# Set attention and SoLU MLP in one kernel: the finish and the norm on ScalarE and GpSimd, the output weights spread by TensorE, and batch 0's turned x stored once all x is in

## The chip, the cores and the metric

The kernel runs on one core of a Trainium2 chip, as one hand-ordered program. The time is device time in microseconds of one execution; three runs of the kernel before took 1380.73 to 1383.75 us, median 1381.25.

The engines are named as the profile names them: PE is TensorE's matmul stream and PEld its weight loads, DVE is VectorE, ACT ScalarE, POOL GpSimd, SP SyncE, which here only issues transfers.

## What is computed

Four batches of 12608 rows of 128 values go through an attention block with 32 inducing points and then through a SoLU MLP with a layer norm. Everything is float32; the weights `w_in`, `w_out` and `g_ln` arrive as 64-bit floats.

```python
def mab(q, kv):                                  # softmax attention, scale 1/sqrt(128)
    s = scale * (q @ kv.transpose(0, 2, 1)); s = s - s.max(-1, keepdims=True)
    a = np.exp(s); a /= a.sum(-1, keepdims=True) + 1e-09
    return a @ kv
h = mab(I, x)            # 32 points look at all rows of a batch
x1 = mab(x, h)           # every row looks at the 32 pooled points
h = x1 @ w_in                                    # 128 -> 1024
e = np.exp(h - h.max(-1)); solu = h * e / (e.sum(-1) + 1e-09)
ln = (solu - mean(solu)) / np.sqrt(var(solu) + 1e-06) * g_ln
out = ln @ w_out                                 # 1024 -> 128
```

## The kernel before

**Tiles and stages.** A tile is 128 rows; a batch has 99 tiles (the last one half full), so there are 396 tiles in all. Groups of four tiles share one product with the output weights; five groups share one finish, so there are 100 groups and 20 finishes.

- `p1(b, k)` reads a chunk of x (up to 12 tiles in batch 0, 16 later), turns it on PE (L614 in batch 0, L583 later), copies it out (`xT`, L561, L593), stores the turned chunk to the DRAM tile `xd` (L624), and updates a running softmax of the 32 points over all rows. `combine(b)` makes the pooled points `h4` and `hs = h4 @ w_in` (L767 to L793).
- `p2(b, j)` takes up to 16 tiles, reads the turned x back from `xd` (L818), makes the scores of the rows against the pooled points (L833), their softmax numerators (L840 to L852), turns those (L875, L889) and computes `rn`, minus the reciprocal of their sums: L908 sums, L911 negates and adds 1e-9, L914 inverts.
- `main` with `mm1` multiplies a tile of numerators with `hs` (L1013). `soft` evicts the 128x1024 product from PSUM on DVE (L1054), takes the exponential on ACT (L1065), multiplies on POOL (L1069), squares on ACT for the norm's sums (L1080) and turns the result on DVE (L1093). `products` and `driver` multiply the turned groups with the output weights `wc` on PE (L1136), in two halves (`w`) that can run beside each other and beside L1013. `evacuate` copies the result out on DVE or ACT (L1159).
- `floor` carries the row sums through DRAM into the layout of the result (L1110, L1118). `finish(b, f)` makes the norm's factor for five groups: L1185 to L1189 on DVE, a logarithm and an exponential on ACT (L1192, L1193), L1196 to L1198 on DVE, all on tiles of 128x20 values. Then POOL scales five groups (L1205) and `stored` writes them (L1217, L1231).

**The start.** `rounded` turns a 64-bit weight matrix into float32 with integer operations on DVE (L417 to L426), one conversion on ACT (L428), multiplications and additions on POOL (L431, L433), a mask on DVE (L435) and a multiplication by it on POOL (L438). `weights_in` and `weights_out` use the same five work buffers (`conv`, part of the `EU` buffers and `hn_b[1]`), one after the other. `weights_out` then scales by the gain (ACT, L460), subtracts the mean of the rows (PE L469, DVE L474) and copies each 32-row block of the result to four places with 16 transfers (L490), which makes `wc`.

**What sets the order.** A planner (`Planner.run`) steps through a model of the engines at build time and emits each instruction when the model has its inputs ready, the lowest priority number first. Each engine's queue is thus a fixed order. The constants at the top (`PR_...`, `P1_...`, `WOUT`, `WIN`, `LATE`) are priorities, and `HN_MORE`, `EUS` and `MINE` share out buffers: four spare buffers of 128x1024 are split between `HN` (evicted products) and `EU` (exponentials), and `MINE` bounds how many first products may be under way.

**Banks.** In the start the eight PSUM banks are `bank_e`, in the locks `EARLY_TR` and `EARLY_PB`. `handover` closes them and gives out four double banks `H` once all of batch 0's `p1` and `hs` are done. Until then nothing that needs `H` can run, neither `mm1` nor, before the change, `p2(0, 0)`.

Of the kernel before, what the change touches and what calls it, by code (L numbers as in the profile page):

```python
# [55 lines left out]
HN_MORE = 3  # L56
RAWS = 2
FILL = 400
FIRST = 4
LATE = -15  # L60
P1_FROM = 3
P1_GO = -20
P1_STEP = 11
P2_AHEAD = 35
P2_START = 35
PR_EX = -2
PR_EV = -20
PR_FI = 40
PR_G2 = 4
PR_HN = -4  # L70
PR_MU = 1
PR_SQ = 1
PR_TU = 4
# [177 lines left out]
def set_attention_then_solu_kernel(ctx: ExitStack, tc: tile.TileContext, x, inducing, w_in, w_out, g_ln, out):  # L251
# [9 lines left out]
    start = min(FIRST, some[0][1] - 1)  # L261
    at_groups = [[(0, start), (start, some[0][1] - start)] + some[1:]] + [some] * (NB - 1)
# [66 lines left out]
    HW = Lock([(buf([C, P], f"h4_{i}"), buf([P, FF], f"hs{i}")) for i in range(2)])  # L329
# [75 lines left out]
    def rounded(dst, src, w, after, free, prio):  # L405
        flat = w[0].bitcast(U32)
        raw = flat.rearrange("p (f two) -> p f two", two=2)
        bits, rest, power, mag = (v.bitcast(U32) for v in w[1:])
        lo, hi = raw[:, :, 0], raw[:, :, 1]
        to = flat if len(src.shape) == 2 else flat.rearrange("p (k d) -> p k d", k=KC)  # L410
        got = (yield after["raw"]) if after else None
        d = yield dma(P * FF * 8, lambda: nc.sync.dma_start(to, src), got, prio=prio)
        ts, stt = nc.vector.tensor_scalar, nc.vector.scalar_tensor_tensor
        gt, gs = nc.gpsimd.tensor_tensor, nc.gpsimd.tensor_scalar
        keep = power.bitcast(F32)
# [6 lines left out]
        a = yield Op("DVE", 1100, lambda: stt(out=bits, in0=hi, scalar=0xC0000000, in1=bits, op0=ALU.bitwise_and, op1=ALU.bitwise_or), a)  # L422
# [12 lines left out]
        k = yield Op("DVE", 602, lambda: ts(out=keep, in0=mag.bitcast(I32), scalar1=float(0x38100000), scalar2=None, op0=ALU.is_ge), g)  # L435
        plan.set(free["mag"], k)
        for c in cuts:
            g = yield Op("POOL", 1180, lambda: gt(out=dst[:, c], in0=dst[:, c], in1=keep[:, c], op=ALU.mult), g, k)  # L438
# [10 lines left out]

    def weights_out():  # L450
        wg2 = hn_b[2]
        wg = wg2.rearrange("p (k d) -> p k d", k=KC)
        g = yield from rounded(wg2, w_out.bitcast(U32).rearrange("(k p) d -> p k d", p=P), conv, conv_free, conv_end, WOUT)
# [3 lines left out]
        gd = yield dma(4096, lambda: nc.sync.dma_start(g_sb, g_ln.rearrange("(k p) -> p k", p=P)))  # L457
# [6 lines left out]
        g = [d]  # L464
        mp, rel = yield H
# [5 lines left out]
        d = yield Op("PE", KC * 215, mean, g, rel, prio=LATE)  # L471
# [54 lines left out]
    e2 = [wc_flat[:, 2 * each : 2 * each + PG0 * M], wc_flat[:, 2 * each + PG0 * M : 2 * each + 2 * PG0 * M]] + [spare[:, (5 * PG0 * C) + i * PG0 * M :][:, : PG0 * M] for i in range(2)]  # L526
# [4 lines left out]
    turned = [Event() for _ in range(NP[0])]  # L531

    def p1(b, k):
# [86 lines left out]
        yield copied  # L620

        def store():
# [3 lines left out]
            d = yield dma(n * P * C * 4, go, ready)  # L626
# [179 lines left out]
    def p2(b, j):  # L806
        s0, n = at_groups[b][j]
        A = aT_of[(b, j)]
        bank = H
        prev = []  # L810
        for k, (g0, gn) in enumerate(p1_groups[b]):
            if g0 < s0 + n and s0 < g0 + gn:
                d = yield xd_done[(b, k)]
                prev += d
        xT, rel = yield X2
        d = yield dma(
            n * P * C * 4,
            lambda: nc.sync.dma_start(xT[:, :n, :].rearrange("p s t -> p (s t)"), xT_dram[b][:, s0 * P : (s0 + n) * P]),  # L818
            rel, prev,
        )  # L820
# [17 lines left out]
        d = yield Op("PE", SWITCH + n * 60, scores, d, rel, hd)  # L838
        give(X2, xT, d)
# [17 lines left out]
        ways, copied, read = [0, 1], [], []  # L857

# [50 lines left out]
        d = yield Op(
            "DVE", 75,  # L910
            lambda: nc.vector.tensor_scalar(out=nr[:, :n], in0=nr[:, :n], scalar1=-1.0, scalar2=-1e-9, op0=ALU.mult, op1=ALU.add),  # L911
            d,
        )
# [254 lines left out]
    def finish(b, f):  # L1168
# [16 lines left out]
        de = yield small(lambda: ts(out=z, in0=S, scalar1=1e-3, scalar2=1e-12, op0=ALU.mult, op1=ALU.add), fd)  # L1185
        de = yield small(lambda: tt(out=z, in0=z, in1=z, op=ALU.mult), de)  # L1186
        d = yield small(lambda: stt(out=part, in0=total, scalar=1.0 / (FF * FF), in1=total, op0=ALU.mult, op1=ALU.mult), F["out"])  # L1187
        d = yield small(lambda: tt(out=v, in0=Q, in1=part, op=ALU.subtract), fd, d)
        d = yield small(lambda: stt(out=v, in0=v, scalar=0.0, in1=z, op0=ALU.max, op1=ALU.add), d, de)  # L1189

        def inverse():
            nc.scalar.activation(y, v, AF.Ln)  # L1192
            nc.scalar.activation(root, y, AF.Exp, scale=-0.5)  # L1193

        da = yield Op("ACT", 330, inverse, d)
        d = yield small(lambda: stt(out=z, in0=root, scalar=-0.5, in1=root, op0=ALU.mult, op1=ALU.mult), da)  # L1196
        d = yield small(lambda: tt(out=z, in0=z, in1=v, op=ALU.mult), d)  # L1197
        dy = yield small(lambda: stt(out=y, in0=z, scalar=1.5, in1=root, op0=ALU.add, op1=ALU.mult), d, da)  # L1198
# [52 lines left out]
    def handover():  # L1251
# [6 lines left out]
        done += d  # L1258
        bank_pool.__exit__(None, None, None)
# [63 lines left out]
```

## Time and profile before

| what | us |
|---|---|
| median of three runs | 1381.25 |
| the profiled execution | 1387.33 |
| its span, first to last instruction | 1385.1 |
| PE busy / PEld busy | 1236.7 / 1142.9 |
| DVE busy | 1255.2 |
| ACT busy | 1062.2 |
| POOL busy | 1072.8 |

The page gives each engine's busy time over the whole span, then groups of instructions by line, with the buffers written and read, the shape, the count, the busy time and the mean duration of one, and after a bar the idle time of the engine just before them and who ended it. "Busy" means that an instruction has begun and not ended; an instruction that sits on an engine and waits for a resource counts as busy too. PE's matmuls overlap, and one float32 matmul leaves two records, so a count of PE records per microsecond says more than its busy share. The table of stretches gives the same busy times for any part of the span, with the granted PE clock as a share of full speed.

### The profile page before, as it was taken

Reading aid. Unit: us, or ns where it says so; the run is one execution under the profiler, and the core shown is the slowest. Engines: PE = TensorE matmul, PEld = TensorE weight load, DVE = VectorE, ACT = ScalarE, POOL = GpSimd, SP = SyncE. Lnnn points to the kernel's source line nnn. Section 1 sums busy time; section 2 is a strip of 40 time slices with the busy share of each in tenths; the row PEclk is TensorE's granted clock in tenths of the full one; section 3 lists DMA queues with packets and bytes.
Section 4 is the critical chain, followed back from the end, with each engine's and each line's share of the span. In section 5 each row is a group of like instructions: output and inputs, shape, how many; then the busy total and the mean of one; then the engine's idle time right before and its main releaser. Section 6 shows DMA issues by size and latency. Waiting matters only on the chain. (4 is left out here: it accounts for less than half of the span.)

```text
span 1385.1 us, 77913 instructions
## 1 busy us (share of the span) xinstructions
PE 1236.7 (89%) x35557; PEld 1142.9 (83%) x35557; DVE 1255.2 (91%) x1882; ACT 1062.2 (77%) x2015; POOL 1072.8 (77%) x557
## 2 busy tenths in 40 slices
PE   9889999989988989899989998689998998989785
PEld 7678888978887978888878887688888887889784
DVE  5698899999999899999998999999999899999992
ACT  5588688968877877878887787578787787789681
POOL 2577587959876978878887778678788796889793
PEclk9879899999999999999999999899999999999897
DMA  9552242203231325312213324121222020201102
GB/s 365 187 162 65 82 138 65 85 17 103 60 123 50 100 65 156 87 44 55 82 45 123 117 78 125 47 88 30 67 70 73 4 70 19 63 4 43 31 16 75
DMA packets 152905, 113.58 MB, mean 82 GB/s; under 512 B 76256, under 2 KB 132608, under 8 KB 148096
## 3 DMA queue, kind: packets, MB, share of 16 engines
q1 hardware_dynamic: 152576, 108.62, 26.2%
q8 instruction: 277, 4.54, 1.4%
q14 instruction: 52, 0.43, 0.1%
HBM read 54.30 MB, written 52.18 MB: 77 GB/s over the span
## 5 line engine op out<-in xcount | busy, mean ns | idle before, releaser
L1136 PE MATMUL h<-wc,vt 32*128 32x129 f32 x25600 | 1068.9, 280 | 34.0 <-issue 17.1
L1136 PEld LDWEIGHTS h<-wc,vt 32*128 32x128 f32 x25600 | 1023.8, 191 | 71.3 <-issue 40.5
L1013 PE MATMUL h<-hs,aT 32*128 32x128 f32 x6336 | 459.6, 286 | 81.0 <-DVE spare L1054 46.6
L1069 POOL TENSOR_TENSOR eu<-hn,eu 128x1024 f32<-128x1024 f32 x197 | 463.3, 2372 | 77.4 <-ACT eu L1065 75.5
L1013 PEld LDWEIGHTS h<-hs,aT 32*128 32x128 f32 x6336 | 408.0, 196 | 109.1 <-DVE spare L1054 53.5
L1093 DVE STREAM_TRANSPOSE vt<-eu 128x1024 f32<-128x1024 f32 x330 | 402.6, 1228 | 1.3 <-POOL eu L1069 1.0
L1080 ACT ACTIVATE sq<-eu 128x1024 bf16<-128x1024 f32 x330 | 347.2, 1052 | 31.0 <-POOL eu L1069 25.5
L1069 POOL TENSOR_TENSOR eu<-spare,eu 128x1024 f32<-128x1024 f32 x133 | 313.7, 2375 | 58.8 <-ACT eu L1065 56.0
L1054 DVE TENSOR_SCALAR_CACHE_REDUCE hn<-h,rn 128x1024 f32<-128x1024 f32 x198 | 248.6, 1261 | 29.7 <-PE h L1013 20.5
L1054 DVE TENSOR_SCALAR_CACHE_REDUCE spare<-h,rn 128x1024 f32<-128x1024 f32 x198 | 248.8, 1260 | 25.8 <-PE h L1013 23.2
L1065 ACT ACTIVATE eu<-hn,nm 128x1024 f32<-128x1024 f32 x197 | 224.9, 1143 | 25.4 <-DVE hn L1054 19.6
L1069 POOL TENSOR_TENSOR spare<-spare 128x1024 f32<-128x1024 f32 x65 | 154.2, 2372 | 31.6 <-ACT spare L1065 31.4
L1065 ACT ACTIVATE eu<-spare,nm 128x1024 f32<-128x1024 f32 x133 | 151.9, 1143 | 24.8 <-DVE spare L1054 20.4
L1205 POOL TENSOR_TENSOR spare<-spare,fin 128x512 f32<-128x512 f32 x100 | 101.0, 1042 | 46.7 <-issue 32.1
L1159 ACT COPY spare<-h 128x258 f32<-128x258 f32 (+1 forms) x119 | 43.7, 371 | 112.1 <-PE h L1136 111.6
L1093 DVE STREAM_TRANSPOSE vt<-spare 128x1024 f32<-128x1024 f32 x66 | 80.8, 1225 | 0.3 <-POOL spare L1069 0.2
L1065 ACT ACTIVATE spare<-spare,nm 128x1024 f32<-128x1024 f32 x65 | 74.3, 1143 | 4.1 <-DVE spare L1054 3.7
L1080 ACT ACTIVATE sq<-spare 128x1024 bf16<-128x1024 f32 x66 | 69.3, 1050 | 4.9 <-POOL spare L1069 3.8
L1080 ACT ACTIVATION_READ_ACCUMULATOR sq<-eu 128x1 f32 x330 | 62.7, 190 | 0.0
L1159 DVE COPY spare<-h 128x258 f32<-128x258 f32 (+1 forms) x81 | 32.7, 410 | 33.1 <-PE h L1136 32.7
L583 PE MATMUL h<-ident,xn 32*128 32x32 f32 x1188 | 54.3, 227 | 6.6 <-DVE spare L1054 3.7
L845 POOL TENSOR_TENSOR s<-s,mx 128x512 f32<-128x512 f32 (+3 forms) x29 | 26.7, 922 | 42.4 <-DVE mx L842 41.3
(162 smaller groups left out, 971.5 us busy)
## 6 DMA issues: line engine op xcount, KB each, us to landing
out_dram<-spare SPq DMA_DIRECT2D x96, 256.0 KB, 3.7
xT<-xd SPq DMA_DIRECT2D x19, 1024.0 KB, 5.4
xn<-in_x_dram SPq DMA_DIRECT2D x15, 1024.0 KB, 6.6
xd<-xT SPq DMA_DIRECT2D x15, 1024.0 KB, 4.7
dl<-dd SPq DMA_DIRECT2D x396, 1.0 KB, 2.6
xd<-vt SPq DMA_DIRECT2D x7, 768.0 KB, 10.4
spare<-in_x_dram SPq DMA_DIRECT2D x5, 768.0 KB, 12.5
xT<-xd SPq DMA_DIRECT2D x5, 768.0 KB, 4.4
```

Of the source, the lines that this page charges most:

```text
L583: nc.tensor.transpose(out=tr[:, k * 512 + s * M : k * 512 + (s + 1) * M], in_=xn[r, s, :], identity=ident[r, r])
L845: lambda: nc.gpsimd.tensor_tensor(out=s2[:, :n, :], in0=s2[:, :n, :], in1=mx[:, :n].unsqueeze(2).to_broadcast([P, n, M]), op=ALU.subtract),
L1013: nc.tensor.matmul(hp[:, cols], lhsT=aT[rows, i // 2, :], rhs=hs[rows, cols], start=True, stop=True)
L1054: lambda: nc.vector.tensor_scalar(out=hn, in0=hp, scalar1=rn, scalar2=None, op0=ALU.mult, op1=ALU.min, accum_out=nm),
L1065: "ACT", 1133, lambda: nc.scalar.activation(e, hn, AF.Exp, bias=nm, scale=-1.0, accum_out=G["qe"][:, s, 1:2]), d, rel, srel,
L1069: d = yield Op("POOL", 2330, lambda: nc.gpsimd.tensor_tensor(out=e, in0=hn, in1=e, op=ALU.mult), de, prio=t + PR_MU)
L1080: "ACT", 1040, lambda: nc.scalar.activation(sq, e, AF.Square, scale=1.0 / 32.0, accum_out=G["qe"][:, s, 0:1]), d,
L1093: lambda: nc.vector.transpose(out=G["vtb"][:, : n * FF].rearrange("p (j s t) -> p j s t", j=M, s=n)[:, :, s, :], in_=e.rearrange("p (a f) ...
L1136: nc.tensor.matmul(op[:rows, a - 2 * w, : C + 1], lhsT=vt[q, k, :], rhs=wc[q, k, :], start=(k == 0), stop=(k == JB - 1))
L1159: return lambda: eng(F["raw"][:rows, i0 : i0 + 2, :], op[:rows, :, : C + 1])
L1205: return lambda: eng.tensor_tensor(out=raw, in0=raw, in1=y[:, i0 : i0 + 4].unsqueeze(2).to_broadcast([rows, 4, C]), op=ALU.mult)
```

## The change

- `finish`: the eight DVE instructions go. Squares, the clamp and two linear steps are done on ACT, two-input steps on POOL: five small ACT instructions beside the two that were there (L1192, L1193), and four on POOL.
- `p2`: the negation of the row sums (L911) is an ACT instruction.
- `rounded`: the mask and the multiplication by it become one DVE instruction; the two POOL halves go.
- `weights_out` gets work buffers of its own (`conv2`, lent by `HW`, `A4`, `AT` and `HN`), is loaded ahead of `w_in`, and replaces the 16 transfers by eight matmuls with `fold2`, which copy each 32-row block to the four places, and eight copies out of PSUM on ACT or DVE. Its mean and these products use the early banks, and `handover` waits for `wc`.
- `p1` of batch 0 stores its turned chunks only when all loads of batch 0 have landed. The first chunk of batch 0 (12 tiles) is cut for `p2` into 4 and 8 tiles that read `xT` where it is in SBUF. `p2(0, 0)` runs in the early banks and turns its numerators whole.
- Constants: `HN_MORE` 3 to 4 (seven `HN` and five `EU` buffers in place of six and six), `MINE` 2 to 3, `WINDOW_TILES` 3 to 4, and several priorities.

```diff
-HN_MORE = 3
+HN_MORE = 4
...
-PR_HN = -4
-PR_MU = 1
-PR_SQ = 1
-PR_TU = 4
+PR_HN = 0
+PR_MU = -4
+PR_SQ = 4
+PR_TU = 12
...
-WINDOW_TILES = 3
-MINE = 2
+WINDOW_TILES = 4
+MINE = 3
...
+WOUT_X = -17.5
 WOUT = -8
-WIN = -18.5
+WIN = -15.5
...
-        k = yield Op("DVE", 602, lambda: ts(out=keep, in0=mag.bitcast(I32), scalar1=float(0x38100000), scalar2=None, op0=ALU.is_ge), g)
-        plan.set(free["mag"], k)
-        for c in cuts:
-            g = yield Op("POOL", 1180, lambda: gt(out=dst[:, c], in0=dst[:, c], in1=keep[:, c], op=ALU.mult), g, k)
+        g = yield Op(
+            "DVE", 1150,
+            lambda: stt(out=dst, in0=mag.bitcast(I32), scalar=float(0x38100000), in1=dst, op0=ALU.is_ge, op1=ALU.mult), g, m,
+        )
...
-        mp, rel = yield H
+        yield turned[NP[0] - 1]
+        mp, rel = yield EARLY_PB.at(LATE)
...
-        for a in range(4):
-            for q in range(4):
-                c = yield dma(
-                    M * FF * 4,
-                    lambda: nc.sync.dma_start(rows[a * M : (a + 1) * M, :, q, :C], wg[q * M : (q + 1) * M]), d, o, issue=600, prio=LATE,
-                )
...
+            def copies():
+                for q, sp in enumerate(four):
+                    r = slice(q * M, (q + 1) * M)
+                    nc.tensor.matmul(sp, lhsT=fold2[r, :], rhs=wg2[r, k0 * C : (k0 + half) * C], start=True, stop=True)
...
+            dc = yield Op(
+                "ACT", 570, out_of(nc.scalar.copy, sp, q, k0), dp, o, prio=LATE,
+                alt=Op("DVE", 620, out_of(nc.vector.tensor_copy, sp, q, k0), dp, o, prio=LATE),
+            )
...
+            here = []
+            for e in loaded if early else ():
+                d = yield e
+                here += d
+            d = yield dma(n * P * C * 4, go, ready, here)
...
+        if b == 0 and s0 + n <= PG0:
+            rel = yield early_xT["ready"]
+            xT = early_xT["tile"][:, s0 : s0 + n, :]
+            d = rel
...
-        d = yield Op(
-            "DVE", 75,
-            lambda: nc.vector.tensor_scalar(out=nr[:, :n], in0=nr[:, :n], scalar1=-1.0, scalar2=-1e-9, op0=ALU.mult, op1=ALU.add),
-            d,
-        )
+        d = yield Op("ACT", 100, lambda: nc.scalar.activation(nr[:, :n], nr[:, :n], AF.Copy, scale=-1.0, bias=-1e-9), d)
...
-        de = yield small(lambda: ts(out=z, in0=S, scalar1=1e-3, scalar2=1e-12, op0=ALU.mult, op1=ALU.add), fd)
-        de = yield small(lambda: tt(out=z, in0=z, in1=z, op=ALU.mult), de)
-        d = yield small(lambda: stt(out=part, in0=total, scalar=1.0 / (FF * FF), in1=total, op0=ALU.mult, op1=ALU.mult), F["out"])
-        d = yield small(lambda: tt(out=v, in0=Q, in1=part, op=ALU.subtract), fd, d)
-        d = yield small(lambda: stt(out=v, in0=v, scalar=0.0, in1=z, op0=ALU.max, op1=ALU.add), d, de)
+        gt, act = nc.gpsimd.tensor_tensor, nc.scalar.activation
+        dz = yield Op("ACT", 135, lambda: act(z, S, AF.Square, scale=1e-3, bias=tiny[:rows]), fd)
+        d = yield Op("ACT", 135, lambda: act(part, total, AF.Square, scale=1.0 / FF), F["out"])
+        d = yield Op("POOL", 205, lambda: gt(out=v, in0=Q, in1=part, op=ALU.subtract), fd, d)
+        d = yield Op("ACT", 135, lambda: act(v, v, AF.Relu), d)
+        d = yield Op("POOL", 205, lambda: gt(out=v, in0=v, in1=z, op=ALU.add), d, dz)
...
+            act(z, root, AF.Square)
...
-        d = yield small(lambda: stt(out=z, in0=root, scalar=-0.5, in1=root, op0=ALU.mult, op1=ALU.mult), da)
-        d = yield small(lambda: tt(out=z, in0=z, in1=v, op=ALU.mult), d)
-        dy = yield small(lambda: stt(out=y, in0=z, scalar=1.5, in1=root, op0=ALU.add, op1=ALU.mult), d, da)
+        d = yield Op("POOL", 205, lambda: gt(out=z, in0=z, in1=v, op=ALU.mult), da)
+        d = yield Op("ACT", 135, lambda: act(z, z, AF.Copy, scale=-0.5, bias=1.5), d)
+        dy = yield Op("POOL", 205, lambda: gt(out=y, in0=z, in1=root, op=ALU.mult), d)
...
+        for e in (early_turned, wc_ready):
+            d = yield e
+            done += d
         bank_pool.__exit__(None, None, None)
```

More of the change, by code (lines that the diff above doesn't have):

```diff
@@ L260, in set_attention_then_solu_kernel @@
     some = cut(NT, AG, GS)
-    start = min(FIRST, some[0][1] - 1)
-    at_groups = [[(0, start), (start, some[0][1] - start)] + some[1:]] + [some] * (NB - 1)
+    start = min(FIRST, PG0 - 1)
+    first = [(0, start), (start, PG0 - start)]
+    at_groups = [first + [(PG0 + s, n) for s, n in cut(NT - PG0, AG, GS)]] + [some] * (NB - 1)
     NP, NG = [len(g) for g in p1_groups], len(ff_groups)
@@ L456, in weights_out @@
         give(HN, hn_b[1], g)
-        gd = yield dma(4096, lambda: nc.sync.dma_start(g_sb, g_ln.rearrange("(k p) -> p k", p=P)))
+    def weights_out():
+        gd = yield dma(4096, lambda: nc.sync.dma_start(g_sb, g_ln.rearrange("(k p) -> p k", p=P)), prio=WOUT_X)
+        wg2 = hn_b[2]
+        wg = wg2.rearrange("p (k d) -> p k d", k=KC)
+        for lock, bufs, at in ((HW, hw_b, ("raw",)), (A4, [a4_b], ("bits",)), (AT, aT_b, ("rest", "mag")), (HN, hn_b[:1], ("power",))):
+            spawn(lend(lock, bufs, *[conv2_free[k] for k in at]), WOUT)
+        g = yield from rounded(wg2, w_out.bitcast(U32).rearrange("(k p) d -> p k d", p=P), conv2, None, conv2_free, WOUT_X)
         def gain(k):
@@ L493, in weights_out, with out_of @@
-        give(HN, wg2, *spread)
-        plan.set(wc_ready, *o_end, *spread)
+        give(EARLY_PB, mp, d)
+        freed = []
+        for k in range(2):
+            got = yield p1_done[0][k]
+            freed += got
+        o = yield Op("POOL", 200, lambda: nc.gpsimd.memset(wc[:, :, C : C + 1], 1.0), freed)
+        rows = wc.rearrange("p (k q) d -> p k q d", q=4)
+        half = KC // 2
+        last, laid = [], [o]
+        def out_of(eng, sp, q, k0):
+            return lambda: eng(rows[:, k0 : k0 + half, q, :C], sp.rearrange("p (k d) -> p k d", k=half))
@@ new lines, in laid_out, with spread @@
+        def laid_out(sp, q, k0, dp):
+            dc = yield Op(
+                "ACT", 570, out_of(nc.scalar.copy, sp, q, k0), dp, o, prio=LATE,
+                alt=Op("DVE", 620, out_of(nc.vector.tensor_copy, sp, q, k0), dp, o, prio=LATE),
+            )
+            give(EARLY_PB, sp, dc)
+            laid.append(dc)
+            if len(laid) == 9:
+                plan.set(wc_ready, *laid)
+        def spread(k0):
+            four, free = [], []
+            for q in range(4):
+                sp, rel = yield EARLY_PB.at(LATE)
+                four.append(sp)
+                free += rel
+            def copies():
+                for q, sp in enumerate(four):
+                    r = slice(q * M, (q + 1) * M)
+                    nc.tensor.matmul(sp, lhsT=fold2[r, :], rhs=wg2[r, k0 * C : (k0 + half) * C], start=True, stop=True)
+            dp = yield Op("PE", 1200, copies, d, free, prio=LATE)
+            last.append(dp)
+            if len(last) == 2:
+                give(HN, wg2, *last)
+            for q, sp in enumerate(four):
+                spawn(laid_out(sp, q, k0, dp), LATE)
@@ L496, in fill @@
+        for k0 in (0, half):
+            spawn(spread(k0), LATE)
     def fill(bank):
@@ L525, in set_attention_then_solu_kernel @@
     EARLY_T = Lock([vt_all[:, i * each : (i + 1) * each].rearrange("p (s t) -> p s t", t=P) for i in range(3 * GS * FF // each)] + [xT_b[:, :PG0, :]])
-    e2 = [wc_flat[:, 2 * each : 2 * each + PG0 * M], wc_flat[:, 2 * each + PG0 * M : 2 * each + 2 * PG0 * M]] + [spare[:, (5 * PG0 * C) + i * PG0 * M :][:, : PG0 * M] for i in range(2)]
+    e2 = [spare[:, 5 * each + i * PG0 * M :][:, : PG0 * M] for i in range(4)]
     EARLY_EW = Lock([(e2[i], e2[i + 1].rearrange("p (s m) -> p s m", m=M)) for i in (0, 2)] + [(ew_b[0][:, : PG0 * M], ew_b[1][:, :PG0, :])])
@@ L531, in set_attention_then_solu_kernel @@
     turned = [Event() for _ in range(NP[0])]
+    loaded = [Event() for _ in range(NP[0])]
+    early_turned = Event()
+    early_xT = {"tile": None, "ready": Event(), **{s0: Event() for s0, n in at_groups[0] if s0 + n <= PG0}}
     def p1(b, k):
@@ L547, in p1 @@
                 xd.append((d, c0))
+        if early:
+            plan.set(loaded[k], *[d for d, at in xd])
         if k == 0:
@@ L619, in p1 @@
             plan.set(turned[k])
-        yield copied
+        got = yield copied
+        if early and not k:
+            early_xT["tile"] = xT
+            plan.set(early_xT["ready"], *got)
         def store():
@@ L808, in p2 @@
         A = aT_of[(b, j)]
[L809 to L819, printed above, removed]
-        )
+        early = b == 0 and j == 0
+        bank = EARLY_PB if early else H
+        if b == 0 and s0 + n <= PG0:
+            rel = yield early_xT["ready"]
+            xT = early_xT["tile"][:, s0 : s0 + n, :]
+            d = rel
+        else:
+            prev = []
+            for k, (g0, gn) in enumerate(p1_groups[b]):
+                if g0 < s0 + n and s0 < g0 + gn:
+                    d = yield xd_done[(b, k)]
+                    prev += d
+            xT, rel = yield X2
+            d = yield dma(
+                n * P * C * 4,
+                lambda: nc.sync.dma_start(xT[:, :n, :].rearrange("p s t -> p (s t)"), xT_dram[b][:, s0 * P : (s0 + n) * P]),
+                rel, prev,
+            )
         hd = yield h_ready[b]
@@ L857, in p2, with turned_whole, turn @@
         ways, copied, read = [0, 1], [], []
+        def turned_whole():
+            tr, trel = yield bank
+            def turn():
+                for q in range(pairs):
+                    both = a4[:, 2 * q : 2 * q + 2].rearrange("t s r m -> t (s r m)")
+                    nc.tensor.transpose(out=tr[:, q * P : (q + 1) * P], in_=both, identity=ident)
+            dt = yield Op("PE", 108.7 * pairs, turn, de, trel)
+            d = yield Op(
+                "ACT", 94 + 96 * pairs,
+                lambda: nc.scalar.copy(aT[:, :pairs, :], tr[:, : pairs * P].rearrange("p (q t) -> p q t", t=P)), dt, rel,
+            )
+            give(bank, tr, d)
+            plan.set(early_turned, d)
+            yield turned_too
+            give(A4, a4, dt, *turned_too.after)
+            for s in range(n):
+                plan.set(aT_ready[(b, s0 + s)], *turned_too.after, d)
+            plan.set(A["all"], d)
         def turned_rows():
@@ L1265, in handover @@
             d = yield xd_done[(0, k)]
+            done += d
+        for s0, n in first:
+            d = yield early_xT[s0]
             done += d
```

76 lines of the change are left out of this document (39 added, 37 removed).

## The prediction

> **What bounds the kernel now.** The page first: which engine is busiest, and what the chain that ended last is made of.
>
> ```profile
> span 1385.1 us, 77913 instructions
> ...
> PE 1236.7 (89%) x35557; PEld 1142.9 (83%) x35557; DVE 1255.2 (91%) x1882; ACT 1062.2 (77%) x2015; POOL 1072.8 (77%) x557
> ...
> PE 19%; DVE 15%; issue 5%; POOL 2%; ACT 1%; POOLq 0%; DVEq 0%; ACTq 0%
> PE h L1136 13%; PE h L1013 5%; DVE vt L1093 4%; DVE hn L1054 3%; DVE spare L1054 2%; DVE nr L911 2%; DVE fin L1185 1%; POOL spare L1205 1%; POOL eu L1069 1%; DVE fin L1186 0%; ACT eu L1065 0%; DVE fin L1187 0%; ACT sq L1080 0%; DVE fin L1197 0%; PE h L833 0%
> ```
>
> DVE leads at 91%. The chain reaches back over only 42% of the span, and in it instructions of a few values, L911 and L1185, stand beside 128x1024 ones. The groups with shapes kept apart say why.
>
> ```profile
> L911 DVE TENSOR_SCALAR nr<-nr 128x16 f32<-128x16 f32 x19 | 34.6, 1819 | 0.0
> L911 DVE TENSOR_SCALAR nr<-nr 128x7 f32<-128x7 f32 x4 | 11.4, 2842 | 0.0
> L911 DVE TENSOR_SCALAR nr<-nr 128x12 f32<-128x12 f32 x5 | 9.1, 1829 | 0.0
> L1185 DVE TENSOR_SCALAR fin<-dl 128x20 f32<-128x20 f32 x20 | 26.1, 1305 | 0.3 <-issue 0.3
> L1186 DVE TENSOR_TENSOR fin<-fin 128x20 f32<-128x20 f32 x20 | 24.1, 1207 | 0.2
> L1187 DVE SCALAR_TENSOR_TENSOR fin<-spare 128x20 f32<-128x20 f32 x20 | 11.4, 571 | 0.0
> L1188 DVE TENSOR_TENSOR fin<-dl,fin 128x20 f32<-128x20 f32 x20 | 14.7, 734 | 0.3
> L1189 DVE SCALAR_TENSOR_TENSOR fin<-fin 128x20 f32<-128x20 f32 x20 | 15.6, 781 | 0.3
> L1196 DVE SCALAR_TENSOR_TENSOR fin<-fin 128x20 f32<-128x20 f32 x20 | 11.1, 553 | 0.5 <-ACT fin L1193 0.5
> L1197 DVE TENSOR_TENSOR fin<-fin 128x20 f32<-128x20 f32 x20 | 9.0, 449 | 0.1
> L1198 DVE SCALAR_TENSOR_TENSOR fin<-fin 128x20 f32<-128x20 f32 x20 | 9.4, 469 | 0.2
> ```
>
> The eight finish lines hold 121.4 us of DVE, L911 55.1. Then the timeline, DVE beside POOL, at the longest waits and at the last finish.
>
> ```profile
> 862.99 8.84 DVE L911 TENSOR_SCALAR nr<-nr 128x16 f32<-128x16 f32 x1
> 864.85 6.95 POOL L1069 TENSOR_TENSOR eu<-hn,eu 128x1024 f32<-128x1024 f32 x3
> ...
> 1343.95 7.63 DVE L1185 TENSOR_SCALAR fin<-dl 128x20 f32<-128x20 f32 x1
> 1344.53 7.02 POOL L1069 TENSOR_TENSOR eu<-hn,eu 128x1024 f32<-128x1024 f32 x3
> 1372.65 0.18 DVE L1185 TENSOR_SCALAR fin<-dl 128x20 f32<-128x20 f32 x1
> 1374.84 5.03 POOL L1205 TENSOR_TENSOR spare<-spare,fin 128x512 f32<-128x512 f32 x5 [13.25 <-issue]
> ```
>
> Both small instructions end when a run of POOL multiplications ends (864.85 + 6.95 = 871.80, 1344.53 + 7.02 = 1351.55); with POOL idle the same one takes 0.18. So these 188 instructions are waits for POOL: 176.5 - 188 x 0.18 = 142.7 us, of which 7.5 lie in the tail. Of DVE's 91%, 81 are work and 10 are waiting.
>
> **The change, part by part.** Stretches of the trace give the stock of work and the best rate seen; of the last two rows, which hold L1054 alone, each eviction leaves two records.
>
> ```profile
> 100.00:1340.00 1240.00, 1120.73 (x33499) 1046.03 (x33493) 1163.43 (x1686) 985.86 (x1858) 998.38 (x500) 0.96 0.24 70
> 650.00:700.00 50.00, 48.08 (x1510) 45.38 (x1508) 47.98 (x71) 42.56 (x81) 45.76 (x24) 1.00 0.32 94
> ...
> 100.00:1340.00 1240.00, 480.55 (x763) 0.96 0.24 70
> 650.00:700.00 50.00, 22.65 (x36) 1.00 0.32 94
> ```
>
> The columns are stretch, length, then busy time of PE, PEld, DVE, ACT and POOL (DVE alone in the last two). Between 100 and 1340 us a tile takes 1240 / 381.5 = 3.25 us; in the good stretch from 650 to 700 it takes 50 / 18 = 2.78.
>
> *Finish and norm.* DVE loses 142.7 - 7.5 = 135 us of waiting there: 1163 to 1028. What takes it up:
>
> ```profile
> L845 POOL TENSOR_TENSOR s<-s,mx 128x128 f32<-128x128 f32 x1 | 0.4, 400 | 0.0
> L703 POOL TENSOR_SCALAR l<-l,small 128x1 f32<-128x1 f32 x12 | 4.6, 380 | 21.9 <-ACT eT L694 11.2 <-ACT wc L694 4.8 <-ACT spare L694 4.2
> L1193 ACT ACTIVATE fin<-fin 128x20 f32<-128x20 f32 x20 | 4.4, 219 | 0.6
> ```
>
> POOL gets four instructions per finish. No such one is in the trace; the nearest rows are 0.38 and 0.40, and 0.20 is a floor taken from ACT's 0.22. I take 0.30: 18 finishes in the stretch x 4 x 0.30 = 22 us, POOL 998 to 1020. ACT gets five per finish and one per `p2`: (18 x 5 + 26) x 0.22 = 26 us, 986 to 1012. So DVE, POOL and ACT end within 2% of each other and none hides the others. POOL at the 91.5% of the good stretch gives 1020 / 0.915 = 1115 us; DVE at its present 93.8% gives 1096; PE at 1510 / 50 = 30.2 records per us gives 33499 / 30.2 = 1109. A whole run won't match one good stretch, so I take 1130, POOL at 90%: **-110 us**, 81% of the waits. Bounds: -144 (DVE's 1096) and 0, if other waits fill the gap. New waits: L914 stands on DVE behind an ACT instruction, with the next evictions behind it; POOL's small steps stand behind ACT, with the multiplications behind them. Both are rivals below.
>
> *Order and buffers.* Priorities add no instruction. One `EU` buffer fewer shows against this row:
>
> ```profile
> L1065 ACT ACTIVATE eu<-hn,nm 128x1024 f32<-128x1024 f32 x197 | 224.9, 1143 | 25.4 <-DVE hn L1054 19.6 <-DVE vt L1093 5.4
> ```
>
> ACT waited 5.4 us for a buffer that a turn frees; turns now go later. Between 0 and some 20 us, on an engine at 90%; it is inside the 1130.
>
> *The start.* First the rows of before, in order of time:
>
> ```profile
> 26.37 2.52 POOL L438 TENSOR_TENSOR w_in_sb<-w_in_sb,eu 128x512 f32<-128x512 f32 x2 [1.56 <-DVE small L663]
> ...
> 46.03 0.91 DVE L435 TENSOR_SCALAR eu<-hn 128x1024 f32<-128x1024 int32 x1
> 47.39 0.59 ACT L793 COPY hs<-bank_e 128x512 f32<-128x512 f32 x1 [5.50 <-PE bank_e L790]
> ...
> 53.75 1.28 DVE L1054 TENSOR_SCALAR_CACHE_REDUCE hn<-h,rn 128x1024 f32<-128x1024 f32 x1 [2.62 <-PE h L1013]
> ...
> 56.28 0.32 SPq L818 DMA_DIRECT2D xT<-xd  x1
> ...
> 62.04 1.23 DVE L474 TENSOR_TENSOR hn<-h,hn 128x1024 f32<-128x1024 f32 x1 [2.48 <-PE h L469]
> ...
> 72.41 1.27 DVE L1054 TENSOR_SCALAR_CACHE_REDUCE hn<-h,rn 128x1024 f32<-128x1024 f32 x1
> ...
> 82.69 1.66 PE L1136 MATMUL h<-wc,vt 32*128 32x129 f32 x22 [0.51 <-issue]
> ```
>
> Beside them the evictions up to there, the loads' stretch and the form of the new mask:
>
> ```profile
> 50.00:82.69 32.69, 11.25 (x18) 0.65 0.73 216
> ...
> 10.00:20.00 10.00, 10.00 (x123) 7.27 (x125) 8.30 (x24) 6.66 (x16) 1.23 (x3) 1.00 1.04 392
> ...
> L422 DVE SCALAR_TENSOR_TENSOR eu<-eu 128x1024 uint32<-128x1024 uint32 x2 | 2.4, 1219 | 0.0
> ```
>
> Four tiles come between 53.75 and 72.41, 18.7 us; at 3.25 they take 13. That 5.7 us goes if tiles 4 to 11 read `xT` in SBUF and nothing of the gain, mean and spread stands between. An earlier `wc` is worth little: nine tiles (18 records) were evicted before 82.69 and the three turned buffers hold twelve, so nothing stood behind it yet. Against it: all of `w_out` now comes before the handover. Its DVE work, L435's place (0.91, now 1.22 by L422's form), L474 (1.23) and `w_in`'s longer mask (0.3), moves ahead of the first eviction: 0.91 + 0.3 + 1.23 + 0.3, some 3 us. The eight copies cost 8 x 0.59 by the ACT copy of 128x512 (L793); ACT stood idle 5.5 us ahead of it, which covers them, and without that cover 2 to 5 us come on top. Two POOL instructions of 1.26 (L438) go from each conversion, which were hidden behind DVE. `w_in` lands later by `w_out` and three chunks, 3.4 MB at 392 GB/s or 9 us: its last POOL step moves from 28.9 to 38, still ahead of L793. The stores that are held back until the loads land have time until the reread, at 56.28 before. Net **-3 us**, between -9 and +8.
>
> The Trainium skill, SBUF, "Who interferes with whom", says that DVE and GpSimd share a port pair, that the loser blocks for the whole instruction, and that a DVE instruction with two SBUF inputs is among those that contend. The trace agrees on who waits, not on how long: L1185 waited through three POOL instructions, not one. By that rule the new mask of `rounded` (two SBUF inputs) can still block; at one POOL instruction of 1.26 for each weight the sum would be 2.5 us later.
>
> *The tail.* The 7.63 us of 1343.95 go; then PE's last products are late next. The last finish, 2.2 us from 1372.65 to POOL's scaling at 1374.84, becomes eleven steps: seven on ACT and four on POOL, 7 x 0.22 + 4 x 0.30 + some handing over, about 4. Net **-5 us**, between -7 and +3.
>
> Sum: 1385.1 - 110 - 3 - 5 = 1267 of span, 1269 for an execution (2.2 lie around the span). The profiled execution, 1387.3, stood 6.1 above the median of 1381.25, so **1263**.
>
> **The rivals.**
>
> *PE takes over.* Its records come at 33499 / 1120.7 = 29.9 per busy us. If they pack no better, PE at 95% busy needs 1180 us: -60 in place of -110, **1313**. For it: PE leads the chain, 19% to 15%. Against: the good stretch packs 1510 / 48.1 = 31.4, and PE's clock, 0.96 on average, was 1.00 there; fewer DVE stalls mean fewer pauses. Chance 0.20.
>
> *All is regained.* DVE's share stays at 93.8%: -144, with -7 and -8 at the ends: **1222**. For it: 650 to 700. Against: four engines at 90%. Chance 0.17.
>
> *The waits only move to ACT.* If each of 29 reciprocals finds an ACT instruction (1.14) ahead of the negation, DVE stands 33 us: -77, **1296**. Chance 0.06.
>
> *Slower.* POOL becomes the engine that waits. Its queue is fixed, and each of 72 small steps in the stretch needs an ACT result; if it arrives late by two ACT instructions of 1.14 (L1065) and its own (2.5 us), POOL holds 1020 + 180 = 1200 us, at 91.5% 1311: +71 where -110 was, **1444**. It decides from (1020 + 72 w) / 0.915 = 1240, a wait w of 1.6 us each. Against: ACT has 20% idle. Chance 0.05.
>
> **How the numbers follow.** The forecast has 0.50, the rivals 0.20, 0.17, 0.06 and 0.05; 0.02 is left for a time within 0.2%, which is about what a measurement of this kernel tells from no change. So faster 0.93, same 0.02, slower 0.05. The range 1215 to 1325 takes in PE's and ACT's rivals at their prices and the full gain; it leaves out 0.05 + 0.02, the far end of PE's rival (0.07) and what is under 1215 (0.04).
>
> **What the profile of after would show.** Right: no DVE instruction of under 40 values over 0.5 us; DVE, POOL and ACT at 88 to 92% between 100 and the last 45 us; PE at 29 to 30 records per us; POOL's small steps near 0.3 us with little idle time ahead of them; the fifth eviction about 13 us after the first. Wrong: DVE below 85% with idle time ended by PE L1013 (PE took over), POOL idle for "ACT fin" (the slower case), L914 idle for ACT, or a first eviction after 58 us (the handover waits for `wc`).

## The result and the profile after

| | before | after |
|---|---|---|
| median, us | 1381.13 (1380.73 to 1383.75) | 1276.21 (1274.78 to 1276.44) |
| ratio | | 0.9234 (95%: 0.9218 to 0.9250) |
| span of the profiled execution | 1385.1 | 1274.2 |

The kernel is 104.9 us shorter. 1263 us had been forecast, with 1215 to 1325 as the range. The page of the changed kernel, its busy times and the chain of waits:

```profile
span 1274.2 us, 77833 instructions
...
PE 1202.3 (94%) x35497; PEld 1113.7 (87%) x35497; DVE 1110.8 (87%) x1689; ACT 1086.2 (85%) x2155; POOL 1085.8 (85%) x633
...
PE 54%; ACT 21%; issue 8%; POOL 8%; DVE 7%; DMA 1%; SPq 0%; ACTq 0%; POOLq 0%; DVEq 0%
PE h L1224 36%; PE h L1101 10%; ACT eu L1153 9%; ACT sq L1168 9%; POOL eu L1157 7%; DVE spare L1142 1%; PE h L898 1%; PE h L635 1%; DVE vt L1181 1%; DVE accn L831 1%; PE h L784 1%; ACT spare L1247 1%; PE h L702 1%; POOL spare L1290 1%; ACT aT L978 1%
```

DVE lost 144.4 us of busy time (1255.2 to 1110.8). That this lies close to the 142.7 that had been read as waiting is chance: the lines that went held 176.5 by their own durations, work and overlaps with their neighbours included, and the scaling of the pooled points holds 12 us more than before (15.6, L831, for 3.6, L772). The small instructions of the finish and the norm are gone from the chain. ACT gained 24 us and POOL 13: POOL's small steps were added, and the mask products of the weights fell away. The stretch between the start and the tail shows how the engines now stand to each other (stretch, length, then PE, PEld, DVE, ACT and POOL, the granted clock, and the transfers):

```profile
100.00:1228.00 1128.00, 1080.35 (x33303) 1014.47 (x33296) 1017.28 (x1493) 998.66 (x1971) 1005.68 (x571) 0.98 0.27 77
```

DVE, ACT and POOL are busy for 90, 89 and 89% of it, and PE leaves 33303 / 1128 = 29.5 records per us, where it left 27.0 before. What the finish and the norm now cost, from the groups with shapes kept apart:

```profile
L1269 ACT ACTIVATE fin<-dl,tiny 128x20 f32<-128x20 f32 x20 | 6.0, 299 | 0.1
L1271 POOL TENSOR_TENSOR fin<-dl,fin 128x20 f32<-128x20 f32 x20 | 5.0, 248 | 19.6 <-ACT fin L1270 19.6
L1273 POOL TENSOR_TENSOR fin<-fin 128x20 f32<-128x20 f32 x20 | 4.7, 237 | 6.6 <-ACT fin L1272 6.6
L1001 ACT ACTIVATE nr<-nr 128x16 f32<-128x16 f32 x19 | 4.0, 211 | 2.1 <-DVE nr L1000 2.0
```

A POOL step takes 0.24 to 0.25 us and an ACT step 0.2 to 0.3. POOL stood 19.6 and 6.6 us for ACT ahead of the first two steps (9.0 and 2.9 ahead of the other two), 1.9 us per finish. The evictions mark the parts, in the timeline of DVE: the first, the fifth and the last of the changed kernel, then the last of the kernel before.

```profile
57.22 1.28 DVE L1142 TENSOR_SCALAR_CACHE_REDUCE hn<-h,rn 128x1024 f32<-128x1024 f32 x1 [0.17 <-PE h L1101]
...
67.73 1.28 DVE L1142 TENSOR_SCALAR_CACHE_REDUCE spare<-h,rn 128x1024 f32<-128x1024 f32 x1
...
1235.68 1.24 DVE L1142 TENSOR_SCALAR_CACHE_REDUCE spare<-h,rn 128x1024 f32<-128x1024 f32 x1
```

```profile
1339.94 1.25 DVE L1054 TENSOR_SCALAR_CACHE_REDUCE hn<-h,rn 128x1024 f32<-128x1024 f32 x1
```

| part | before | after | difference |
|---|---|---|---|
| up to the fifth eviction | 72.4 | 67.7 | -4.7 |
| fifth to last eviction | 1267.5 | 1168.0 | -99.6 |
| last eviction to the end | 45.2 | 38.5 | -6.6 |

So nine tenths of the gain lie in the long middle. That the start's edits give none of it is tested below (`moved_alone`).

### The profile page after: what moved, and what is told of

The parts are those of the page before. It is cut to its first block, busy times and chain, and to the rows that moved or that the text cites. A ratio compares the mean times of both kernels' runs of the same rounds, so it can differ in the third digit from the quotient of the medians.

```text
span 1274.2 us, 77833 instructions
## 1 busy us (share of the span) xinstructions
PE 1202.3 (94%) x35497; PEld 1113.7 (87%) x35497; DVE 1110.8 (87%) x1689; ACT 1086.2 (85%) x2155; POOL 1085.8 (85%) x633
## 4 chain that ended last, share of the span: by engine, by line
PE 54%; ACT 21%; issue 8%; POOL 8%; DVE 7%; DMA 1%; SPq 0%; ACTq 0%; POOLq 0%; DVEq 0%
PE h L1224 36%; PE h L1101 10%; ACT eu L1153 9%; ACT sq L1168 9%; POOL eu L1157 7%; DVE spare L1142 1%; PE h L898 1%; PE h L635 1%; DVE vt L1181 1%; DVE accn L831 1%; PE h L784 1%; ACT spare L1247 1%; PE h L702 1%; POOL spare L1290 1%; ACT aT L978 1%
## 5 line engine op out<-in xcount | busy, mean ns | idle before, releaser
L1224 PE MATMUL h<-wc,vt 32*128 32x129 f32 (+1 forms) x25600 | 1034.4, 276 | 24.6 <-issue 15.1
L1224 PEld LDWEIGHTS h<-wc,vt 32*128 32x128 f32 (+1 forms) x25600 | 996.8, 187 | 67.7 <-issue 48.5
L1157 POOL TENSOR_TENSOR eu<-spare,eu 128x1024 f32<-128x1024 f32 x225 | 529.5, 2380 | 51.0 <-ACT eu L1153 50.9
L1181 DVE STREAM_TRANSPOSE vt<-eu 128x1024 f32<-128x1024 f32 x396 | 481.3, 1230 | 16.3 <-POOL eu L1157 15.9
L1168 ACT ACTIVATE sq<-eu 128x1024 bf16<-128x1024 f32 x396 | 416.8, 1052 | 46.0 <-POOL eu L1157 36.4
L1157 POOL TENSOR_TENSOR eu<-hn,eu 128x1024 f32<-128x1024 f32 x171 | 402.6, 2377 | 44.3 <-ACT eu L1153 42.6
L1153 ACT ACTIVATE eu<-spare,nm 128x1024 f32<-128x1024 f32 x225 | 256.6, 1142 | 3.0 <-DVE vt L1181 1.7
L1142 DVE TENSOR_SCALAR_CACHE_REDUCE hn<-h,rn 128x1024 f32<-128x1024 f32 x171 | 214.8, 1263 | 38.1 <-PE h L1101 27.5
L1168 ACT ACTIVATION_READ_ACCUMULATOR sq<-eu 128x1 f32 x396 | 74.8, 189 | 0.0
L635 PEld LDWEIGHTS h<-ident,xn 32*128 32x128 f32 x1188 | 51.9, 143 | 2.3 <-issue 1.5
L645 ACT COPY xT<-h 128x1024 f32<-128x1024 f32 (+2 forms) x42 | 37.8, 901 | 10.6 <-PE h L635 10.1
L1153 ACT ACTIVATION_READ_ACCUMULATOR eu<-spare,nm 128x1 f32 x225 | 42.7, 190 | 0.0
```

Of the source, the lines that this page charges most:

```text
L635: nc.tensor.transpose(out=tr[:, k * 512 + s * M : k * 512 + (s + 1) * M], in_=xn[r, s, :], identity=ident[r, r])
L645: lambda: nc.scalar.copy(xT.rearrange("c s (q t) -> c q s t", q=4)[:, 2 * w : 2 * w + 2, :n, :], tr.rearrange("c (k x) -> c k x", k=2)[:, ...
L1142: lambda: nc.vector.tensor_scalar(out=hn, in0=hp, scalar1=rn, scalar2=None, op0=ALU.mult, op1=ALU.min, accum_out=nm),
L1153: "ACT", 1133, lambda: nc.scalar.activation(e, hn, AF.Exp, bias=nm, scale=-1.0, accum_out=G["qe"][:, s, 1:2]), d, rel, srel,
L1157: d = yield Op("POOL", 2330, lambda: nc.gpsimd.tensor_tensor(out=e, in0=hn, in1=e, op=ALU.mult), de, prio=t + PR_MU)
L1168: "ACT", 1040, lambda: nc.scalar.activation(sq, e, AF.Square, scale=1.0 / 32.0, accum_out=G["qe"][:, s, 0:1]), d,
```

## The experiments

Three questions: is it the waiting of the small DVE instructions; do the new start, the priorities and the buffers carry a part; and what sets the pace now. The runs were made on three chips, four kernels on each. On them the kernel before had medians of 1379.5, 1377.6 and 1379.8, with single runs from 1363 to 1394, so a few microseconds between kernels of different chips say nothing.

### Put back on DVE, and moved alone

`finish_back` has the eight instructions of the finish on DVE again:

```diff
-        dz = yield Op("ACT", 135, lambda: act(z, S, AF.Square, scale=1e-3, bias=tiny[:rows]), fd)
...
+        de = yield small(lambda: ts(out=z, in0=S, scalar1=1e-3, scalar2=1e-12, op0=ALU.mult, op1=ALU.add), fd)
...
```

> The changed kernel with the eight finish instructions on DVE again; all else as changed. If waiting for POOL was the cost, the wait comes back as in the kernel before, 92.6 us or somewhat more since POOL is now busy a larger share of the time, and four fifths of it show in the time: 1276 + 75, 1340 to 1365 us. Rival, the gain came from the new priorities and buffers: under 1300 us, the eight lines wait but other engines cover it.

`norm_back` has the negation of the row sums there:

```diff
-        d = yield Op("ACT", 100, lambda: nc.scalar.activation(nr[:, :n], nr[:, :n], AF.Copy, scale=-1.0, bias=-1e-9), d)
+        d = yield Op(
+            "DVE", 75,
+            lambda: nc.vector.tensor_scalar(out=nr[:, :n], in0=nr[:, :n], scalar1=-1.0, scalar2=-1e-9, op0=ALU.mult, op1=ALU.add),
+            d,
+        )
```

> The changed kernel with the negation of the row sums on DVE again. If waiting for POOL was the cost, 29 waits of 1.8 us or more come back, 50 us or more of DVE, and 1276 + 40 = 1310 to 1330 us. Rival, priorities and buffers: under 1290 us.

`both_back` has both edits:

> Both back on DVE, with the new start, priorities and buffers kept. By the theory of waits nearly all of the gain goes: 1276 + 105 to 115, 1370 to 1395 us. Rival, priorities, buffers and the new start carry half of the gain: 1310 to 1345 us.

`moved_alone` goes the other way: the kernel before, with only these two parts of the change made.

> The kernel before with nothing changed but the finish and the norm, both off DVE. By the theory of waits most of the gain is there without the rest: 1381 - 95, 1275 to 1300 us. Rival, the new priorities and buffers are what let the other engines use the time: over 1320 us.

| kernel | median, us | ratio to before (95%) |
|---|---|---|
| finish_back | 1372.95 | 0.9993 (0.9957 to 1.0030) |
| norm_back | 1316.31 | 0.9498 (0.9421 to 0.9575) |
| both_back | 1396.39 | 1.0102 (1.0042 to 1.0162) |
| moved_alone | 1269.77 | 0.9193 (0.9127 to 0.9258) |

The theory of waits holds at both ends. With both parts back on DVE nothing of the gain is left, and the two parts alone, in the old kernel with its old start, order and buffers, give all of it: 0.9193 and 0.9234 have overlapping intervals. Everything else in the change together is worth nothing that these runs can show, and without the two parts it costs 1%.

The size came out larger than expected for the finish, +97 us where 64 to 89 was written down, and as expected for the norm, +40. Both are taken from the 1276.21 of the changed kernel, which ran on another chip; by the ratios they are about 105 and 36. The groups of `finish_back` go some way to say why; its waits are longer than in the kernel before (105 us for 92.6):

```profile
L1273 DVE TENSOR_SCALAR fin<-dl 128x20 f32<-128x20 f32 x20 | 37.3, 1867 | 0.1
L1274 DVE TENSOR_TENSOR fin<-fin 128x20 f32<-128x20 f32 x20 | 16.7, 835 | 0.3
L1275 DVE SCALAR_TENSOR_TENSOR fin<-spare 128x20 f32<-128x20 f32 x20 | 17.3, 867 | 0.0
L1276 DVE TENSOR_TENSOR fin<-dl,fin 128x20 f32<-128x20 f32 x20 | 16.4, 820 | 0.3
L1277 DVE SCALAR_TENSOR_TENSOR fin<-fin 128x20 f32<-128x20 f32 x20 | 16.0, 801 | 0.2
L1284 DVE SCALAR_TENSOR_TENSOR fin<-fin 128x20 f32<-128x20 f32 x20 | 9.7, 487 | 0.7 <-ACT fin L1281 0.5
L1285 DVE TENSOR_TENSOR fin<-fin 128x20 f32<-128x20 f32 x20 | 8.9, 447 | 0.0
L1286 DVE SCALAR_TENSOR_TENSOR fin<-fin 128x20 f32<-128x20 f32 x20 | 11.9, 596 | 0.1
```

The eight lines sum to 134.2 us; less 160 x 0.18 that is 105 of waiting, and 97 of it show in the time: 0.92 us per us. In `norm_back` the negation holds DVE for 49.7 us, 45 of them waiting, and 40 show. The times don't add up (97 + 40 = 137, both together 120), and neither do the waits: in the trace of `both_back` the negation holds DVE for only 27.5 us, and all 189 instructions wait 136 us, not 105 + 45. So there, too, 0.9 us show per us of waiting (120 / 136).

### The wait, or the instruction?

A small instruction between the evictions could cost by its place, whatever it waits for. `norm_accum` has the negation on DVE in the form that also writes an accumulator; the 1e-9 beside the sums is left out:

```diff
+    nmost = buf([P, 1], "nmost")
...
-        d = yield Op("ACT", 100, lambda: nc.scalar.activation(nr[:, :n], nr[:, :n], AF.Copy, scale=-1.0, bias=-1e-9), d)
+        d = yield Op(
+            "DVE", 122,
+            lambda: nc.vector.tensor_scalar(
+                out=nr[:, :n], in0=nr[:, :n], scalar1=-1.0, scalar2=None, op0=ALU.mult, op1=ALU.max, accum_out=nmost
+            ),
+            d,
+        )
```

> The changed kernel with the negation of the row sums on DVE, in the form that also writes an accumulator (the form of L663, 0.20 us each in the kernel before); the 1e-9 beside the sums is left out. If what costs is the wait for POOL, and this form doesn't wait: 29 instructions of 0.2 us or less and the time of the changed kernel within 1%. Rival, a small instruction on DVE costs because it stands between the evictions, whatever its form: 1300 us and more, as with the norm put back.

It took 1277.49 us (1267.84 to 1279.41), ratio 0.9286 (0.9241 to 0.9331). The changed kernel, run again beside it, took 1271.79.

> The changed kernel once more, unchanged, on the chip of the three beside it, as their yardstick: 1260 to 1280 us.

Six runs of it lay between 1259.56 and 1276.03, ratio 0.9245 (0.9196 to 0.9295). The views of the tile `nr` in the two kernels with the negation on DVE, duration minimum, median and maximum in ns; first the plain form of `norm_back`, then the other:

```profile
L1003 DVE TENSOR_SCALAR nr<-nr x29: 129/767/8157, 53.9 to 1219.4; 128x16 f32<-128x16 f32 x19, 128x12 f32<-128x12 f32 x4, 128x7 f32<-128x7 f32 x3, 128x4 f32<-128x4 f32 x1
```

```profile
L1004 DVE TENSOR_SCALAR_CACHE_REDUCE nr<-nr x29: 119/131/170, 53.8 to 1185.4; 128x16 f32<-128x16 f32 x19, 128x12 f32<-128x12 f32 x4, 128x7 f32<-128x7 f32 x3, 128x4 f32<-128x4 f32 x1
```

Same engine, same place in the kernel, same shapes: up to 8.16 us in one form, never over 0.17 in the other, and the time follows the form. It is the wait. The norm need not have left DVE at all. One thing helped this kernel: L831's instruction held DVE for 6.9 us in its profiled execution, and for 15.4 in that of the changed kernel beside it, so a cost of a few microseconds may be hidden, but not one of 40.

That the wait is for POOL can be read from the ends of the instructions. In the kernel before, the finish and the norm have 189 small instructions on DVE (the prediction's 188 and one of four columns). Of these 85 take over 0.3 us, and each of the 85 ends 25 to 56 ns after an instruction of POOL has ended; the other 104 take 0.16 us on average. In `norm_back` it is 21 of 29, with ends 26 to 33 ns after POOL's.

### The constants

`old_constants` is the changed kernel with thirteen constants as before:

```diff
-HN_MORE = 4
+HN_MORE = 3
...
-MINE = 3
+MINE = 2
...
-WINDOW_TILES = 4
+WINDOW_TILES = 3
```

> The changed kernel with the thirteen priorities and buffer counts of before (HN_MORE, FILL, LATE, P1_FROM, P1_STEP, the PR_ numbers, WINDOW_TILES, MINE); new finish, norm and start. Theory: the constants are worth little once the waits are gone, 1262 to 1290 us. Rival: the new buffers and order are tuned to the new balance of engines and carry a part, over 1300 us.

1262.29 us, ratio 0.9200 (0.9123 to 0.9276), inside the expected 1262 to 1290 at its lower end. These priorities and buffers carry none of the gain.

### What sets the pace now

Three kernels keep the order of the changed kernel and take work from one engine: a product left out where `k % 8 == 4`, the product of L1157 on 896 columns, the square of L1168 on 512.

```diff
-            nc.tensor.matmul(op[:rows, a - 2 * w, : C + 1], lhsT=vt[q, k, :], rhs=wc[q, k, :], start=(k == 0), stop=(k == JB - 1))
+            if k % 8 != 4:
+                nc.tensor.matmul(op[:rows, a - 2 * w, : C + 1], lhsT=vt[q, k, :], rhs=wc[q, k, :], start=(k == 0), stop=(k == JB - 1))
...
-nc.gpsimd.tensor_tensor(out=e, in0=hn, in1=e, op=ALU.mult)
+nc.gpsimd.tensor_tensor(out=e[:, :896], in0=hn[:, :896], in1=e[:, :896], op=ALU.mult)
...
-nc.scalar.activation(sq, e, AF.Square, scale=1.0 / 32.0, accum_out=G["qe"][:, s, 0:1])
+nc.scalar.activation(sq[:, :512], e[:, :512], AF.Square, scale=1.0 / 32.0, accum_out=G["qe"][:, s, 0:1])
```

> The changed kernel in the same order, but an eighth of the products with the output weights is left out (4 of every 32 matmuls), so the result lacks them; PE has 1600 of 12800 of these matmuls less to do, about 88 us if four run beside each other. If PE now sets the pace: 40 to 80 us less than 1276. If DVE, POOL and ACT share the limit with it: 5 to 30 us less.

> The changed kernel in the same order, but the product on GpSimd covers 896 of 1024 columns, so an eighth of the result is left unmultiplied; POOL has 396 x 0.28 = 112 us less to do. If POOL sets the pace: 50 to 100 us less than 1276. If PE does: under 20 us less.

> The changed kernel in the same order, but the square for the norm's sums covers 512 of 1024 columns, so the variance is of half of them; ACT has 396 x 0.43 = 170 us less to do. If ACT sets the pace with the others: 20 us or more less than 1276. If PE alone does: under 10 us less.

| kernel | work taken, us, as estimated | busy time less by the profile, us | median, us | against 1276 / 1272 |
|---|---|---|---|---|
| pe_eighth | 88 of PE | 45 | 1245.99 | -30 / -26 |
| pool_eighth | 112 of POOL | 106 | 1253.92 | -22 / -18 |
| act_half | 170 of ACT | 154 | 1263.48 | -13 / -8 |

These stood on another chip than the changed kernel's own runs, so both of its medians are given. Of the busy time that is taken from it, PE gives back some two thirds (a third of the estimate, which PE's overlapping matmuls make uncertain), POOL a sixth to a fifth, ACT less than a tenth. PE is the one that counts most. By the bounds written down, PE's 26 to 30 us say that it shares the limit with others, while POOL's 18 to 22 lie about the bound of 20 and ACT's 8 to 13 about that of 10, so those two decide little. The chains by engine, first with an eighth of PE's products gone, then with an eighth of POOL's:

```profile
POOL 41%; PE 21%; ACT 17%; issue 10%; DVE 6%; DMA 3%; SPq 0%; POOLq 0%; ACTq 0%; DVEq 0%
```

```profile
PE 63%; ACT 19%; DVE 6%; issue 6%; DMA 3%; POOL 2%; SPq 1%; POOLq 0%; ACTq 0%; DVEq 0%
```

With PE relieved POOL takes the chain over; with POOL relieved PE, which had led before, keeps it. Each chain is that of one execution, and in `after_again`, the same kernel as the changed one, it reached back over only 11% of the span (PE 8% of it), so the shares are rough. One row spoils the POOL figure: L831 stood 2.7 us on DVE in the profiled execution of `pool_eighth` and 15.6 in the changed kernel's, which leads to the next experiment. By what that one gives, up to half of POOL's 18 to 22 us may be L831's.

### The wait that the change left

A third instruction of the waiting kind stayed on DVE: the scaling of the pooled points (L772 before). Its view in the kernel before, then in `old_constants`, then in the changed kernel:

```profile
L772 DVE TENSOR_SCALAR accn<-acc,small x4: 310/796/1715, 44.1 to 985.7; 128x128 f32<-128x128 f32 x4
...
L831 DVE TENSOR_SCALAR accn<-acc,small x4: 289/592/2399, 53.4 to 905.8; 128x128 f32<-128x128 f32 x4
...
L831 DVE TENSOR_SCALAR accn<-acc,small x4: 278/3401/8533, 50.1 to 943.6; 128x128 f32<-128x128 f32 x4
...
  PEld h L833: 12.9, 2
  PE h L833: 12.5, 2
```

In the changed kernel it holds DVE for up to 8.53 us, twice with PE standing behind it. The sums of the four are 3.6, 3.9 and 15.6 us. With the old constants the wait was short in every profiled execution (2.8 in `moved_alone`); with the new ones it was 15.6 and 15.4 in the changed kernel's two, and anything from 2.7 to 17.5 where one more edit was made. `accn_act` moves it to ACT:

```diff
-        d = yield Op("DVE", 200, lambda: nc.vector.tensor_scalar(out=accn, in0=acc, scalar1=rl, scalar2=None, op0=ALU.mult), d, prev)
+        d = yield Op("ACT", 250, lambda: nc.scalar.activation(accn, acc, AF.Copy, scale=rl), d, prev)
```

> The changed kernel with the scaling of the pooled points (L831, 15.6 us on DVE in four instructions, 12 us of PE waiting behind two of them) on ACT. If this is the wait that the change left: 8 to 14 us less than the changed kernel beside it. Rival, it is hidden by the tiles in flight: within 4 us.

`old_const_accn` has the constants of before as well:

> The changed kernel with the thirteen constants of before and the scaling of the pooled points on ACT. L831 stood only 3.9 us on DVE under those constants, so at most 4 us less than the kernel with the old constants alone: 1255 to 1264 us, the shortest of all if the constants cost something. Rival, the constants make no difference and the gain is L831's alone: the same time as the kernel before this one in the list, within 3 us.

`accn_act` took 1262.89 us (1261.60 to 1270.47), 8.9 under the changed kernel beside it, as expected; single runs of the two still overlap, so the size is not firm. The four instructions take 1.6 us on ACT. `old_const_accn` took 1254.34 us (1252.03 to 1259.74), ratio 0.9138 (0.9098 to 0.9178): 17.5 under the changed kernel, with six runs against six that hardly touch (its slowest 1259.74, the other's fastest 1259.56). It is the shortest of the kernels that do all of the work, 0.7 below the expected 1255 to 1264 and 8.6 under `accn_act`, so with L831's wait gone the new constants cost something. The rival of equal times fell. The expectation of at most 4 us from L831 under the old constants can't be settled: `old_constants` had run on another chip, 8 us above.

## Why the prediction was right

- **The waits.** 142.7 us of DVE's busy time had been read as waiting for POOL. `moved_alone`, `both_back` and `norm_accum` show that removing these waits was the gain, and the ends of the 85 long instructions that POOL was what they waited for.
- **The middle.** -110 had been forecast and -99.6 came, at the shares that were named: DVE, POOL and ACT at 88 to 92% (measured 89 to 90), PE at 29 to 30 records per us (29.5). The mechanism was right, and the term was 10% too large for the kernel as a whole. What is missing seems to have come with the constants, which the prediction had put "inside the 1130": with the old ones the same stretch, fifth to last eviction, lasted 1153.1 us in `moved_alone` (-114.4) and 1151.4 in `old_constants`, each in one profiled execution (that of `moved_alone` was the fastest of its four runs). Part of it is L831, which as an instruction of the waiting kind belonged on the list: its wait grew to 15.6 us, and taking it away gave some 9, a size that isn't firm. `old_const_accn` against `accn_act` shows a second part, 8.6 us, whose cause stays open.
- **POOL's small steps.** 0.30 us had been taken, 0.24 was measured. The slower rival, POOL waiting 1.6 us or more ahead of every step, did not come: 38 us over all 80 steps, 0.5 each, which is more than the "little idle time" that was to be seen.
- **L914 behind ACT.** DVE stood 0.3 us there in all; that rival fell.
- **PE takes over.** Half true. PE leads the chain with 54% and is busy for 96% of the stretch, but it packs better than the rival assumed: 30.8 records per busy us, where 29.9 had been taken over. The granted clock rose with it, 0.96 to 0.98; no run here tells how much of the packing, or of the gain, is the clock's. `pe_eighth` shows that PE counts most, and that POOL leads once PE has less to do.
- **The start.** -3 had been forecast, -4.7 came up to the fifth eviction, from the two parts named: the first eviction 3.5 us later (57.22 for 53.75), the four tiles after it in 10.5 us where 18.7 were needed and about 13 forecast. In `moved_alone`, with the old start, the fifth eviction came at 71.0. The delay of the first was put down to the DVE work of `w_out`; the last rows of this text show waits in the conversion as well. The new mask (L441) took 2.10 us in one conversion, beside POOL's products, and 1.18 in the other. Behind the fifth eviction nothing of the 4.7 can be told from the rest: `moved_alone` is not slower.
- **The tail.** -5 forecast, -6.6 measured.
- **The offset.** 6.1 us had been taken off because the profiled execution of before stood that far above the median. The profiled execution after (1276.1) stood at its median, so the offset belonged to that one execution and not to the kernel. That is 6 of the 13 us between 1263 and 1276; the smaller gain of the middle, less what the ends gave on top, is the other 7.

Not tried: the parts of the start one by one (the stores held back, the spread by TensorE, the chunk read in SBUF).

## What to carry to other kernels

Look at the duration of the smallest instructions by shape: an instruction of 20 values that takes 1.3 us on average and 7.6 at most is a wait under another name, and a busy share hides it. Put such work where it doesn't wait, which can be another engine or another form on the same engine, and list every instruction of the kind, since a new order can make one that is left wait longer: 15.6 us for 3.6 here, with POOL's share of the time about the same as in `old_constants` (85 and 86%), where it waited 3.9. When four engines stand at 90% or more, less work on one of them gives back only a part of it, here from under a tenth (ACT) to some two thirds of the busy time (PE).

## What the hardware showed that was not expected

Two kinds of wait stand behind POOL. In the finish of the kernel before, the instruction with one tensor input waited through whole runs of POOL's multiplications; those with two tensor inputs never longer than about one of them (2.37 us each):

```profile
L1185 DVE TENSOR_SCALAR fin<-dl x20: 107/862/7629, 154.7 to 1372.6; 128x20 f32<-128x20 f32 x20
L1186 DVE TENSOR_TENSOR fin<-fin x20: 127/1201/2334, 156.5 to 1372.9; 128x20 f32<-128x20 f32 x20
L1187 DVE SCALAR_TENSOR_TENSOR fin<-spare x20: 149/182/2400, 158.7 to 1373.0; 128x20 f32<-128x20 f32 x20
```

It was so in `finish_back` too: 6.49 us at most for the first kind, 2.41 for the second. The longest waits of the plain one-input form were 9.14 us (L911 before), 8.53 (L831 after) and 8.16 (`norm_back`). Not every small instruction of that form waits: L743 of the changed kernel, 30 times on one value per row, never took over 0.16 us.

In the start the loss goes both ways. With the two conversions side by side, DVE's and POOL's instructions of the changed kernel are longer than those of the same shape apart:

```profile
L423 DVE TENSOR_SCALAR eu<-eu 128x1024 uint32<-128x1024 uint32 x1 | 1.8, 1773 | 0.0
L423 DVE TENSOR_SCALAR a<-hs 128x1024 uint32<-128x1024 uint32 x1 | 0.7, 687 | 0.0
L435 POOL TENSOR_TENSOR hn<-hn,hn 128x512 f32<-128x512 f32 x2 | 3.5, 1759 | 0.5 <-ACT hn L432 0.5
L437 POOL TENSOR_TENSOR w_in_sb<-w_in_sb,eu 128x512 f32<-128x512 f32 x2 | 2.5, 1274 | 0.0
```

L423 takes 1.77 us against POOL's multiplications (L435) and 0.69 without. Those take 1.76 us each against DVE's conversion; the additions of the same shape (L437) take 1.27 without it, and in the kernel before the multiplication, too, took 1.27 (L431).
